# A two-layer convolution with a joint network on one core: first loads in a new order, tap 0 in two column parts, a leading tile of 456 columns, and a table of priority corrections

## The chip, the cores and the metric

The kernel runs on one core of one Trainium2 chip. The metric is device time of one execution in microseconds (us). Engines are named as in the profile: PE is TensorE (PEld its weight loads), DVE is VectorE, ACT is ScalarE, POOL is GpSimd, and SP is SyncE, whose queue issues every DMA of this kernel. The profiler was on for one execution; its span runs from the first instruction to the last.

## The reference

The input x has 2 sequences of 4000 samples with 512 channels. All tensors are bfloat16.

```python
B, T, D, K = 2, 4000, 512, 5;  U = 8
xp = jnp.pad(x, ((0,0),(pad,pad),(0,0)))                  # pad = 2
h = sum over i of einsum("btc,cd->btd", xp[:, i:i+T, :], w1[i])
h = gelu(h)[:, ::2, :]                                    # 2000 positions are kept
f = the same with hp = pad(h), w2
f = gelu(f)[:, ::2, :]                                    # 1000 positions are kept
fe = einsum("btd,de->bte", f, w_f);  ge = einsum("bud,de->bue", g, w_g)
j = tanh(fe[:, :, None, :] + ge[:, None, :, :])           # 2 x 1000 x 8 x 512
return einsum("btud,dv->btuv", j, w_o)
```

So there are two convolutions of five taps and stride 2, a small projection, a tanh over 16,000 rows of 512, and a 512 x 512 product on all of these rows.

## The kernel before

Everything is kept with channels on the 128 partitions (four groups of channels, index k) and positions along the row. The work runs in this order.

1. *The leading tile.* The first 2 x NA = 432 outputs of the first convolution in sequence 0 are made by plain products: for each tap (order 0, 4, 2, 1, 3) and each group m of 128 output channels, four products over k (`direct`, with the moving columns from `both`). All four banks of PSUM stay open over the five taps. The samples for it come as rows (`load_xr`, tiles `xr`, two blocks: 128 rows and the rest), are transposed by PE against `ident` (line 501 of the profile), and copied to `xs` by DVE (first block) or ACT (second block). A block holds samples in four phases (position modulo 4); the index pp says even or odd phases, and each block is transposed in two groups, pp = 0 and pp = 1. Taps 0, 4 and 2 read even phases only, taps 1 and 3 odd ones. Eight products on zeros (`warm_mm`, `NWARM`) go ahead of it on PE.
2. *The Triples.* The other outputs of the first convolution and the whole second one are made three output phases at a time by nine products in place of fifteen. Two Triples of N3 = 262 columns finish sequence 0 of the first convolution (inputs `xq`), two of 334 make sequence 1 (`xp`), and two make the second convolution (`hT`). They need sums of weights (`w1part`, `w2part`: tiles `ssum`, `w_x`, `w_t`) and sums of samples (`step`: tiles `row`, `xq`), made by DVE and ACT. Their samples come by transposing DMAs (`load_x6`, line 456 of the profile).
3. *The joint.* After the projection `fe` the tanh rows are made by ACT, and the last product is done in blocks of two by two with seven half-size products in place of eight (class `Seven`) and some plain tiles (`Plain`). The sums that a block of seven needs (line 912, tiles `ss`) run on DVE or POOL, whichever the planner picks; PSUM is emptied by DVE and ACT (`sn`, `og`, `ost`).

The order on each engine is not written by hand. Every step is an operation in a `Plan` with an engine (or a choice of two, `flex`), the tiles it reads and writes, and an assumed cost. `schedule` walks through the operations in assumed time: it takes the engine that is free first and, among operations that are ready, on PE, SP and POOL the one that comes first in the program, on DVE and ACT the one with the earliest due time `late`. Operations made while `pl.pin` is true (up to the end of the leading tile) keep the program's order on their engine. `emit` then writes each engine's fixed list with the semaphore waits that the order needs. Before the change the plan has 1631 operations.

DMAs of weights of the first convolution are held back so that few are under way: `load_w1` makes a load wait, on SP, for the landing of an earlier one (`came[-3]`). What stands behind it in SP's queue waits too, the transposed loads among them.

Of the kernel before, what the change touches and what calls it, by code (L numbers as in the profile page):

```python
# [50 lines left out]
class Psum:  # L51
# [4 lines left out]
        return View(self.h[:, lo:lo + n], np.unique(np.arange(lo, lo + n) // 512), True)  # L56

    def pair(self, lo, step, n):
        ap = self.h[:, lo:lo + 2 * step].rearrange("p (s c) -> p s c", s=2)[:, :, 0:n]
        cells = np.unique(np.concatenate([np.arange(lo, lo + n), np.arange(lo + step, lo + step + n)]) // 512)  # L60
        return View(ap, cells, True)


class Op:
    __slots__ = ("eng", "fn", "reads", "writes", "dma", "signal", "count", "sem", "val", "idx", "cost", "pin", "after", "wire", "alt", "port")


class Plan:
# [88 lines left out]
    def schedule(self, pred):  # L157
# [10 lines left out]
        for i in range(n - 1, -1, -1):  # L168
            t = min([late[s] - (HOP if pred[s][i] else ops[i].cost - span[i]) for s in succ[i]], default=0.0)
            if ops[i].eng == "pe":  # L170
                t = min(t, nextpe)
            late[i] = t - span[i]
            if ops[i].eng == "pe":
                nextpe = late[i]
        left = [len(p) for p in pred]
        ready = [0.0] * n
        free = {e: 0.75 for e in ("pe", "act", "dve", "pool", "sp")}
# [11 lines left out]
        for _ in range(n):  # L189
            best = None  # L190
            for e, c in cand.items():
                if c:
                    t = max(free[e], min(ready[i] for i in c))
                    if best is None or t < best[0]:
                        best = (t, e)
            t, e = best
            now = [i for i in cand[e] if ready[i] <= t + 0.02]
            i = min(now, key=(lambda i: i) if e in ("pe", "sp", "pool") else (lambda i: (late[i], i)))
            for f in engines(i):
                cand[f].remove(i)  # L200
            order[e].append(i)
            o = ops[i]
            if o.alt:
                o.eng, (o.fn, o.cost), o.alt = e, o.alt[e], None
            start[i] = t
            free[e] = t + o.cost
            if o.port:
                if lock > t - 0.2 and e == "dve":
                    free[e] = max(t, lock) + o.cost + 0.2
                elif lock > t:  # L210
                    free[e] = lock + o.cost
                lock = free[e]
            end = free[e]
            if o.dma:
                wire = max(wire, t + 1.8) + o.wire
                end = max(wire, t + 2.0)
            for s in succ[i]:
                ready[s] = max(ready[s], end + HOP if pred[s][i] else free[e])
                left[s] -= 1
                if not left[s]:  # L220
                    for f in engines(s):
                        cand[f].append(s)
# [79 lines left out]
def bass_standalone__seq2seq_rnn_t_joint__speech_kernel(  # L302
# [22 lines left out]
    NK = D // P  # L325
    assert (B, T, D, K, U) == (2, 4000, 512, 5, 8)
    T1, T2 = T // 2, T // 4
    NA, N3 = 216, 262
    NT3 = (T2 + 2) // 3
    XW = 528  # L330
    HOFF, HWID = 2, 338
# [1 line left out]
    RING, WIDE, XB = 12, 10, 24  # L333
    BU = B * U
    NT = 512
    NWARM = 8

    with ExitStack() as es:
        cur = [16512]
# [29 lines left out]
        assert cur[0] <= 229368, cur[0]  # L369
        xp = {i: Buf(nc, f"xp{i}", [6, NK, 352], BF16, xs[i].end - xs[i].bytes) for i in (0, 2)}  # L370
        assert all(xp[i].end <= xs[i].end for i in xp)
        xq = [Buf(nc, f"xq{i}", [6, NK, 288], BF16, v.end - v.bytes) for i, v in enumerate((xs[1], w2_sb))]
        assert xq[0].end <= xs[1].end and xq[1].end <= w2_sb.end
        w1_x = Buf(nc, "w1_x", [3, NK, D], BF16, wf_sb.end - wf_sb.bytes)
        assert w1_x.end <= wo_sb.end
# [30 lines left out]
        def memset(v):  # L406
            pl.op("pool", lambda e: e.memset(v.ap, 0.0), (), (v,))  # L407
# [11 lines left out]
        def mm(o, pairs, start, stop, check=True):  # L419

            def fn(e):
                for n, (l, r) in enumerate(pairs):
                    ins = e.matmul(o.ap, lhsT=l.ap, rhs=r.ap, start=start and n == 0,  # L423
                                   stop=stop and n == len(pairs) - 1, skip_group_check=not check)
                return ins
            pl.op("pe", fn, [v for pr in pairs for v in pr], (o,), len(pairs) * max(o.ap.free_size() / 2400 + 0.0025, 0.1))


        zv = zero[:]
# [12 lines left out]

        NR = (P, NA + 2 - P)

        def load_xr(rt):
            n = NR[rt]
            dst = xr[rt].rows(0, n).map(lambda a: a.rearrange("p r k c -> p (r k c)"))
            src = x[0, 4 * P * rt:4 * (P * rt + n), :].rearrange("(p r) c -> p (r c)", r=4)
            return pl.dma("sp", lambda e: e.dma_start(dst.ap, src), (), (dst,), nbytes=n * 4 * 2 * D)

        def load_x6(buf, b, ph, j0, col, n=336):

            r0 = b * T + 6 * j0 + ph
            dst = buf[ph, :, col:col + n]
            src = x.rearrange("b t d -> (b t) d")[r0:r0 + 6 * (n - 1) + 1:6, :]
            pl.dma("sp", lambda e: e.dma_start_transpose(out=dst.ap, in_=src), (), (dst,), nbytes=n * 2 * D, rate=170e3)  # L456

        came = [load_xr(rt) for rt in range(2)]
        act(warm[0:1], warm[1:2], ACT.Gelu_apprx_tanh)

        def load_w1(i):
            src = w1[i].rearrange("(k c) d -> c k d", c=P)
            if len(came) == 2:
                h = D // 2
                for sl in (slice(0, h), slice(h, D)):
                    o = pl.dma("sp", lambda e, sl=sl: e.dma_start(w1_sb[i, :, sl].ap, src[:, :, sl]), (), (w1_sb[i, :, sl],), nbytes=262144)
            else:
                o = load_w("sp", w1_sb[i], src)
                o.after.append(came[-3].idx)
            came.append(o)  # L470

        def load_xq(i, ph):
            load_x6(xq[i], 0, ph, 2 * NA // 3 + i * N3 - 2, 0, -(-(N3 + 3 - i) // 16) * 16)

        for kind, i in (('w', 0), ('w', 4), ('w', 2), ('w', 1), ('w', 3), ('x', 4), ('x', 0), ('x', 2), ('x', 1), ('x', 3), ('x', 5)):
            if kind == "w":
                load_w1(i)
            else:
                load_xq(0, i)
        for ph in (4, 0, 2, 1, 3, 5):  # L480
            load_xq(1, ph)
        for ph in (4, 0, 2, 1, 3, 5):
            load_x6(xp[2], 1, ph, 0, 16)

        def warm_mm(n):
            o, z, zz = ps.cols(3 * NT, NT), zero[0:P], zero[:]
            for _ in range(n):
                mm(o, [(z, zz)], True, True)
                pl.ops[-1].cost = 0.43

        warm_mm(NWARM)
        psb = ps.h[:, :].bitcast(BF16)
        for rt in range(2):
            for pp in range(2):
                bk, n = 4 + 2 * pp + rt, NR[rt]
                pv = View(psb[:, bk * 1024:(bk + 1) * 1024].rearrange("p (r k c) -> p r k c", r=2, k=NK)[:, :, :, 0:n], np.array([bk]), True)

                def fn(e, rt=rt, pp=pp, pv=pv, n=n):
                    for r in range(2):
                        for k in range(NK):  # L500
                            ins = e.transpose(pv.ap[:, r, k, :], xr[rt].h[0:n, 2 * r + pp, k, :], ident.h[0:n, 0:n])
                    return ins
                pl.op("pe", fn, (xr[rt].rows(0, n), ident[:]), (pv,), 0.55)
                o = xs[0][pp::2, :, 16 + rt * P:16 + rt * P + n]
                if rt:
                    act(o, pv, ACT.Copy)
                else:
                    pl.op("dve", lambda e, o=o, pv=pv: e.tensor_copy(out=o.ap, in_=pv.ap), (pv,), (o,), vec_cost(o, (pv,)))

        def stt(eng, o, a, f, b):  # L510
            pl.op(eng, lambda e: e.scalar_tensor_tensor(  # L511
# [139 lines left out]
        def to_f(b):  # L651
            def out(r, m, src):
# [5 lines left out]
        wb = {"t0": (w2_sb, 0), "s0": (w2_sb, 1), "t1": (w2_sb, 2), "s1": (w2_t, 2), "tm": (w2_t, 0), "t2": (w2_t, 1),  # L658
              "sm": (w2_t, 3), "si": (w2_sb, 3), "ti": (w2_sb, 4)}
        j3 = NA // 3  # L660
        trip = [Triple(xq[0], 2, row[0], wa, to_h(0, j3, N3), N3), Triple(xq[1], 2, row[1], wa, to_h(0, j3 + N3 // 2, N3), N3),
                Triple(xp[2], 16, row[0], wa, to_h(1, 0)), Triple(xp[0], 4, row[1], wa, to_h(1, NT3 // 2)),
                Triple(hT[0], HOFF, row[0], wb, to_f(0)), Triple(hT[1], HOFF, row[1], wb, to_f(1))]

        for b in range(B):
            memset(hT[b][4:6, :, HOFF - 1:HOFF])
            memset(hT[b][:, :, HOFF + NT3:HOFF + NT3 + 2])
        memset(xq[1][0:4, :, 1 + N3:4 + N3])  # L670
        memset(xq[1][4:6, :, N3:4 + N3])
        tap_at = {0: ((2, -1), (0, 0)), 1: ((3, -1), (1, 0)), 2: ((0, 0), (2, 0)),
                  3: ((1, 0), (3, 0)), 4: ((2, 0), (0, 1))}
        taps = (0, 4, 2, 1, 3)

        def both(i, k):

            a, b = (xs[0][r, k, 16 + d:16 + d + NA] for r, d in tap_at[i])
            lo, hi = a.ap, b.ap
            ap = bass.AP(tensor=lo.tensor, offset=lo.offset, ap=[list(lo.ap[0]), [hi.offset - lo.offset, 2], [1, NA]])  # L680
            return View(ap, np.union1d(a.cells, b.cells), False)

        def direct(i, m):
            mm(ps.cols(m * NT, 2 * NA), [(w1_sb[i, k, m * P:(m + 1) * P], both(i, k)) for k in range(NK)],
               i == taps[0], i == taps[-1])

        for i in taps:
            for m in range(NK):
                direct(i, m)
        for m in range(NK):  # L690
            src = ps.pair(m * NT, NA, NA).map(lambda a: a.rearrange("p s (q r) -> p s r q", r=3))
            o = hT[0][:, m, HOFF:HOFF + NA // 3].map(lambda a: a.rearrange("p (r s) q -> p s r q", s=2))
# [434 lines left out]
```

## Time and profile before

| what | value |
|---|---|
| time before, median of 3 runs | 253.12 us (252.08 to 253.51) |
| profiled execution: span | 251.3 us |
| profiled execution: PE busy | 245.7 us (98%) |
| DVE, ACT, POOL busy | 211.8, 210.5, 106.7 us |
| DMA, mean over the span | 127 GB/s |
| DMA from 6 to 12 us | 326 GB/s |
| granted TensorE clock, mean | 1.000 |

The page gives for the profiled execution its span alone, without a device time of its own; the three timed runs lie 0.8 to 2.2 us above that span. A busy share is a share of the span. Matmuls overlap one another in the records (their ends are modelled), so PE's busy time says where PE had work, and the spacing of matmul starts says how fast it went.

### The profile page before, as it was taken

Reading aid. Unit: us, or ns where it says so; the run is one execution under the profiler, and the core shown is the slowest. Engines: PE = TensorE matmul, PEld = TensorE weight load, DVE = VectorE, ACT = ScalarE, POOL = GpSimd, SP = SyncE. Lnnn points to the kernel's source line nnn. Section 1 sums busy time; section 2 is a strip of 40 time slices with the busy share of each in tenths; the row PEclk is TensorE's granted clock in tenths of the full one; section 3 lists DMA queues with packets and bytes.
Section 4 is the critical chain, followed back from the end, with each engine's and each line's share of the span. In section 5 each row is a group of like instructions: output and inputs, shape, how many; then the busy total and the mean of one; then the engine's idle time right before and its main releaser. Section 6 shows DMA issues by size and latency. Waiting matters only on the chain.

```text
span 251.3 us, 5205 instructions
## 1 busy us (share of the span) xinstructions
PE 245.7 (98%) x1920; PEld 184.6 (73%) x1920; DVE 211.8 (84%) x347; ACT 210.5 (84%) x353; POOL 106.7 (42%) x109
## 2 busy tenths in 40 slices
PE   8999999999999999999999999999999999999994
PEld 4556788877666666666467878777788888778873
DVE  1699999967999997971547798999999999999892
ACT  2388699878959869963799999999999999997763
POOL 1000000000000000003338899698998999699930
PEclk9999999999999999999999999999999999999999
DMA  7999999988400052000002223322344336534648
GB/s 212 326 174 176 186 156 208 176 144 274 148 0 3 0 182 71 1 1 3 0 1 85 83 86 127 127 86 83 127 132 164 128 120 219 187 123 148 207 137 266
DMA packets 57392, 31.92 MB, mean 127 GB/s; under 512 B 33837, under 2 KB 57149, under 8 KB 57367
## 3 DMA queue, kind: packets, MB, share of 16 engines
q1 hardware_dynamic: 57367, 31.59, 48.0%
q8 instruction: 15, 0.25, 0.4%
q14 instruction: 10, 0.08, 0.1%
HBM read 7.71 MB, written 16.38 MB: 96 GB/s over the span
## 4 chain that ended last, share of the span: by engine, by line
PE 85%; DMA 6%; DVE 5%; ACT 2%; SPq 1%; issue 1%; DVEq 0%
PE acc L423 85%; DMA xq<-in_x_dram 3%; DMA w_sb<-in_w_dram 2%; DVE row L410 2%; DMA xr<-in_x_dram 1%; DVE xq L410 1%; SPq L456 1%; ACT sn L843 1%; DVE og L410 0%; ACT jT L415 0%; DVE sn L844 0%; DVE ssum L511 0%; ACT ost L843 0%; DVE w_t L410 0%; DVE w_x L410 0%
## 5 line engine op out<-in xcount | busy, mean ns | idle before, releaser
L410 DVE TENSOR_TENSOR og<-acc,sn 128x512 bf16<-128x512 f32 x87 | 56.9, 681 | 3.9 <-PE acc L423 3.1
L415 ACT ACTIVATE jT<-feT,geT 128x1000 bf16<-128x1000 f32 (+6 forms) x56 | 51.7, 975 | 0.5 <-DVE feT L736 0.4
L423 PE MATMUL acc<-tw,ss 128*128 128x256 f16 x348 | 48.0, 273 | 0.0
L912 POOL TENSOR_TENSOR ss<-jT 128x512 f16<-128x512 bf16 x28 | 33.8, 1219 | 12.9 <-ACT jT L415 10.6
L423 PEld LDWEIGHTS acc<-tw,ss 128*128 128x128 f16 x348 | 33.5, 98 | 7.3 <-DVE sn L844 0.3
L843 ACT ACTIVATE sn<-acc 128x512 f32<-128x512 f32 x52 | 31.5, 620 | 3.5 <-PE acc L423 3.2
L423 PE MATMUL acc<-row,w_sb 128*128 128x334 bf16 (+1 forms) x192 | 33.1, 295 | 0.2 <-DVE row L410 0.2
L423 PE MATMUL acc<-wo_sb,jT 128*128 128x256 bf16 (+1 forms) x196 | 31.7, 288 | 0.0
L407 POOL MEMSET hT<- 128x8 bf16 (+2 forms) x6 | 0.7, 148 | 71.8 <-ACT hT L415 66.8
L423 PE MATMUL acc<-row,w_x 128*128 128x262 bf16 (+1 forms) x192 | 28.2, 290 | 0.0
L415 ACT ACTIVATE jX<-feT,geT 128x1000 bf16<-128x1000 f32 (+4 forms) x28 | 25.0, 932 | 0.0
L423 PEld LDWEIGHTS acc<-row,w_sb 128*128 128x128 bf16 x192 | 18.5, 98 | 6.8 <-DVE row L410 0.5
L423 PEld LDWEIGHTS acc<-wo_sb,jT 128*128 128x128 bf16 x196 | 19.2, 98 | 5.3
L423 PEld LDWEIGHTS acc<-row,w_x 128*128 128x128 bf16 x192 | 18.8, 98 | 5.4
L415 ACT ACTIVATE sd<-acc 128x334 f32<-128x334 f32 (+1 forms) x48 | 20.5, 431 | 1.9 <-PE acc L423 1.3
L912 POOL TENSOR_TENSOR ss<-jX 128x512 f16<-128x512 bf16 x18 | 20.9, 1176 | 1.2 <-ACT jX L415 0.7
L415 ACT ACTIVATE hT<-acc 128x262 bf16<-128x262 f32 (+2 forms) x36 | 15.1, 432 | 6.7 <-PE acc L423 6.6
L511 DVE SCALAR_TENSOR_TENSOR acc<-acc,sd 128x334 f32<-128x334 f32 (+1 forms) x24 | 11.6, 483 | 10.4 <-PE acc L423 10.3
L844 DVE COPY sn<-acc 128x512 f32<-128x512 f32 x25 | 16.9, 682 | 2.4 <-PE acc L423 2.2
L423 PE MATMUL acc<-wo_sb,ss 128*128 128x256 bf16 x116 | 17.9, 273 | 0.0
L423 PE MATMUL acc<-hT,w_sb 128*128 128x334 bf16 x96 | 17.4, 305 | 0.0
L912 POOL TENSOR_TENSOR ss<-ss,jT 128x512 f16<-128x512 f16 x14 | 16.4, 1181 | 0.7 <-PE acc L423 0.4
(105 smaller groups left out, 501.6 us busy)
## 6 DMA issues: line engine op xcount, KB each, us to landing
out_dram<-og SPq DMA_DIRECT2D x44, 256.0 KB, 2.3
w_sb<-in_w_dram SPq DMA_DIRECT2D x9, 512.0 KB, 5.0
out_dram<-og SPq DMA_DIRECT2D x14, 128.0 KB, 2.7
out_dram<-ost SPq DMA_DIRECT2D x7, 128.0 KB, 2.0
xr<-in_x_dram SPq DMA_DIRECT2D x1, 512.0 KB, 3.4
w_sb<-in_w_dram SPq DMA_DIRECT2D x2, 256.0 KB, 5.1
wf_sb<-in_w_f_dram SPq DMA_DIRECT2D x1, 512.0 KB, 3.6
wg_sb<-in_w_g_dram SPq DMA_DIRECT2D x1, 512.0 KB, 4.7
```

What stands on the lines that cost most here:

```text
L407: pl.op("pool", lambda e: e.memset(v.ap, 0.0), (), (v,))
L410: pl.op(eng, lambda e: e.tensor_tensor(out=o.ap, in0=a.ap, in1=b.ap, op=op), (a, b), (o,), 0.02 + 2.14e-3 * o.ap.free_size() if eng == "po ...
L415: pl.op("act", lambda e: e.activation(o.ap, i.ap, func, scale=scale, bias=0.0 if bias is None else bias.ap), rd, (o,), o.ap.free_size() * ...
L423: ins = e.matmul(o.ap, lhsT=l.ap, rhs=r.ap, start=start and n == 0, stop=stop and n == len(pairs) - 1, skip_group_check=not check)
L456: pl.dma("sp", lambda e: e.dma_start_transpose(out=dst.ap, in_=src), (), (dst,), nbytes=n * 2 * D, rate=170e3)
L511: pl.op(eng, lambda e: e.scalar_tensor_tensor(out=o.ap, in0=a.ap, scalar=f, in1=b.ap, op0=ALU.mult, op1=add), (a, b), (o,), vec_cost(o, (a ...
L843: pl.flex({"act": (lambda e: e.activation(o.ap, v.ap, ACT.Copy), 0.05 + n * 0.833e-3), "dve": (lambda e: e.tensor_copy(out=o.ap, in_=v.ap) ...
L844: "dve": (lambda e: e.tensor_copy(out=o.ap, in_=v.ap), 0.065 + n * 1.04e-3)}, (v,), (o,))
L912: fn = lambda e, o=S[i], x=x, y=y, op=op: e.tensor_tensor(out=o.ap, in0=x.ap, in1=y.ap, op=op)
```

## The change

Four things change together.

*First loads.* Each `xr` block is loaded in two transfers, even and odd phases. The order on SP becomes: block 0 even, tap 0's weights in two halves of channels (before: two halves of output columns), block 1 even, tap 4, block 0 odd, block 1 odd, taps 2, 1, 3. Tap 2 waits on SP for the landing of tap 4, tap 1 for block 0 odd, tap 3 for block 1 odd.

*Tap 0 in column parts.* After five warm-up products the first group of eight transposes (block 0, even) goes to PE and one more warm-up product follows. Tap 0 is then done for the 128 columns that this block gives (per output half), first for two groups of channels; then come the transposes of block 1 even, the other two groups of channels, and the same for the remaining columns. The transposes of the odd phases move ahead of tap 2. DVE copies both even groups, ACT both odd ones.

*Leading tile of 456 columns.* NA grows from 216 to 228, and the first two Triples have 258 columns for 262.

*A table.* `NUDGES` has one character for each of 1643 operations, from -3.2 to +3.1 in steps of 0.1 us. It is added to the priority by which `schedule` picks among ready operations: to the due time on DVE and ACT, and on SP and POOL to 0.15 times the place in the program. PE keeps the program's order. If the length of the table isn't the number of operations, zeros are used. Some assumed costs are altered as well, and the border memsets of `hT` and `xq` change places in the program.

```diff
+ALPHABET = "0123456789ABCDEFGHIJKLMNOPQRSTUVWXYZabcdefghijklmnopqrstuvwxyz_-"
+NUDGES = (
+    "WWWW ... WWWRP-PwH5QRK_xNvM0mR0_rMrCpnYWK"
...
+        nudge = [0.1 * (ALPHABET.index(c) - 32) for c in NUDGES] if len(NUDGES) == n else [0.0] * n
...
-            i = min(now, key=(lambda i: i) if e in ("pe", "sp", "pool") else (lambda i: (late[i], i)))
+            i = min(now, key=(lambda i: i) if e == "pe" else (lambda i: (0.15 * i + nudge[i], i)) if e in ("sp", "pool") else (lambda i: (late[i] + nudge[i], i)))
...
-    NA, N3 = 216, 262
+    NA, N3 = 228, (258, 258)
...
-    NWARM = 8
+    NWARM = 5
...
-        def load_xr(rt):
+        def load_xr(rt, pp):
             n = NR[rt]
-            dst = xr[rt].rows(0, n).map(lambda a: a.rearrange("p r k c -> p (r k c)"))
-            src = x[0, 4 * P * rt:4 * (P * rt + n), :].rearrange("(p r) c -> p (r c)", r=4)
+            dst = xr[rt].rows(0, n, slice(pp, 4, 2)).map(lambda a: a.rearrange("p r k c -> p r (k c)"))
+            src = x[0, 4 * P * rt:4 * (P * rt + n), :].rearrange("(p r) c -> p r c", r=4)[:, pp::2, :]
...
+        def load_w1(i, parts=1):
+            n = NK // parts
+            for k in range(0, NK, n):
+                src = w1[i, k * P:(k + n) * P].rearrange("(k c) d -> c k d", c=P)
+                dst = w1_sb[i, k:k + n]
+                o = pl.dma("sp", lambda e, dst=dst, src=src: e.dma_start(dst.ap, src), (), (dst,), nbytes=n * 131072)
+                if len(came) > 4:
+                    o.after.append(came[-3].idx)
+                came.append(o)
+
+        came = [load_xr(0, 0)]
+        load_w1(0, 2)
+        came.insert(2, load_xr(1, 0))
         act(warm[0:1], warm[1:2], ACT.Gelu_apprx_tanh)
+        load_w1(4)
+        for rt in range(2):
+            came.append(load_xr(rt, 1))
+        for i in (2, 1, 3):
+            load_w1(i)
...
         warm_mm(NWARM)
+        turn(0, 0, "dve")
+        warm_mm(1)
...
+        for q0, n in ((0, P), (P, NA - P)):
+            for ks in ((0, 1), (2, 3)):
+                for m in range(NK):
+                    mm(ps.pair(m * NT + q0, NA, n), [(w1_sb[0, k, m * P:(m + 1) * P], both(0, k, q0, n)) for k in ks],
+                       q0 == 0 and ks[0] == 0, False, False)
+                if q0 == 0 and ks[0] == 0:
+                    turn(1, 0, "dve")
+        for i in taps[1:]:
+            if i == 2:
+                turn(0, 1, "act")
+                turn(1, 1, "act")
+            for m in range(NK):
+                direct(i, m)
```

`turn(rt, pp, eng)` is the body of the loop over transposes of before as a function: eight transposes of block rt, group pp, on PE, and the copy to `xs` on the engine named.

## The prediction

> **What bounds the kernel now.** I read the page first, then TensorE's timeline of the first 32 us, the chain of waits, and then the waits and the timeline late in the span.
>
> From the page, the span and the busy times:
>
> ```profile
> span 251.3 us, 5205 instructions
> PE 245.7 (98%) x1920; PEld 184.6 (73%) x1920; DVE 211.8 (84%) x347; ACT 210.5 (84%) x353; POOL 106.7 (42%) x109
> ```
>
> PE is the bound. So the question is when its useful work begins, how many columns it streams, and where it stops in between. The timeline of PE alone (start, length, what, in brackets the idle time before it):
>
> ```profile
> 1.19 3.60 PE L423 MATMUL acc<-zero 128*128 128x512 bf16 x8 [1.19 <-DVE zero L430]
> 4.58 2.35 PE L501 MATMUL acc<-ident,xr 128*128 128x128 bf16 x32
> 7.47 14.81 PE L423 MATMUL acc<-xs,w_sb 128*128 128x432 bf16 x80 [0.54 <-ACT xs L415]
> 22.12 3.74 PE L423 MATMUL acc<-row,w_x 128*128 128x262 bf16 x32
> 25.77 1.96 PE L423 MATMUL acc<-xq,w_t 128*128 128x262 bf16 x16
> 27.57 1.06 PE L423 MATMUL acc<-row,w_x 128*128 128x262 bf16 x8
> 28.83 0.62 PE L423 MATMUL acc<-row,w_sb 128*128 128x262 bf16 x4 [0.20 <-DVE row L410]
> ```
>
> Useful products begin at 7.47. The 80 of the leading tile start every (22.12 - 7.47)/80 = 183 ns: 432 columns at 2.4 a nanosecond are 180, and 3 ns on top. I use columns/2.4 + 3 ns below. Between 22 and 29 us 56 products of 262 columns (112 ns, 6.3 us) take 6.7: about 0.45 is lost, most of it before 28.83, where PE waits for DVE.
>
> The same engine's transposes alone, in stretches of 0.6 us (in brackets how many):
>
> ```profile
> 4.60:5.20 0.60, 0.60 (x6) 0.60 (x6) 1.00 1.05 218
> 5.80:6.40 0.60, 0.60 (x14) 0.60 (x12) 1.00 1.19 296
> ```
>
> 128-column transposes come at 107 ns at first and at 56 ns later: PE runs at half rate until about 5.9 us, 4.7 us after its first matmul (the warm-up matmuls too: 3.4 us for eight of 512 columns, 427 ns each), whatever the clock column says.
>
> The chain of waits, in order of time:
>
> ```profile
> 0.74 3.43 DMA xr<-in_x_dram
> 4.19 4.75 DMA w_sb<-in_w_dram
> ...
> 9.37 2.09 SPq L456
> 11.46 0.05 issue
> 11.51 6.42 DMA xq<-in_x_dram
> ...
> 28.83 185.64 PE acc L423 x1464
> ```
>
> Samples, weights and the transposed samples come through one queue; DVE then prepares the first Triple until 28.8, and from there PE sets the end. The last loss is late: the waits between 195 and 235 us, and one DVE instruction beside a POOL instruction there (timeline).
>
> ```profile
> PEld acc L423 <- DVE og L410: 0.7, 1, 0.7
> PEld acc L423 <- DVE sn L844: 0.5, 2, 0.3
> ```
>
> ```profile
> 214.75 2.58 DVE L912 TENSOR_TENSOR ss<-jT,ss 128x512 f16<-128x512 bf16 x1
> 215.90 1.14 POOL L912 TENSOR_TENSOR ss<-jX 128x512 f16<-128x512 bf16 x1
> ```
>
> A sum that takes DVE 0.41 to 0.9 us elsewhere took 2.58 while POOL did sums too. PE's starts then stand 0.54, 0.21 and 0.11 us further apart than their columns need (218.5, 220.4, 226.7); with three small ones late stalls are 0.95 us. Early and late, 1.4 us of stall can be won, no more.
>
> **Part by part.**
>
> *First loads.* Now xr0 (512 KB) lands at 4.17, 3.43 after its issue. Afterwards the first transfer is half of it (256 KB, even phases). Its landing isn't in the trace; the nearest rows are 3.43 us for 512 KB above and 2.0 for a 128 KB store. I take 2.75, so it lands at 3.5 (bounds 2.75 to 4.2). Eight transposes at half rate (107 ns, 0.86 us, the first 0.17 after the landing) end at 4.5; DVE starts 0.24 later, as it does now (5.43 to 5.67), copies for 0.67 (1.33 for two), and 0.06 later PE can go: tap 0 starts at 5.5 (4.75 to 6.2), 2 us earlier. Its weights are the second and third transfer, 768 KB in all by 5.0 at the 350 GB/s at which 512 KB loads now follow each other (1.50 us apart), in time. Tap 4's weights have 0.42 MB less ahead of them: about 1.2 us earlier, 7.7, and PE wants them at 9.3. Taps 2, 1, 3 move behind the odd phases and wait on SP for tap 4 and for these; bytes in all grow by 49 KB (+0.15 us), while rows of 512 bytes disappear (tap 0's halves). So SP comes to the transposed loads at about 9 us, as now (9.37), and I let them land where they do, 17.94 for the second, within 0.6.
>
> *Tap 0 in parts.* 16 products become 32: 16 of 256 columns (110 ns) and 16 of 200 (86 ns), 3.14 us. The right part waits for the second transpose group and its DVE copy: eight transposes after the first eight products, at about 6.6 to 7.0, copy done at 7.8; eight left-part products (0.88) fill that time, so nothing waits. If the copy were 0.5 late, that much would show.
>
> *Transposes inside the stream.* 24 of 32 no longer lie ahead of the products: 8 of 102 columns, 8 of 128, 8 of 102 at 45, 56 and 45 ns, 1.17 us on PE's path. ACT's copies of the odd phases lie beside tap 2, which reads even phases only.
>
> *456 columns.* The other four taps: 64 x 193 ns = 12.35 us. The leading tile costs 3.14 + 12.35 = 15.49 against 14.65: +0.84. The first two Triples have 258 columns for 262: 288 products x 4 columns = -0.48. Their DVE and ACT rows get 1.5% shorter, beside other work.
>
> *Half rate.* 5.5 to 5.9 at half rate costs 0.2. Six warm-up matmuls for eight cost nothing by themselves; they keep the clock busy.
>
> Sum of the front: start -1.97, transposes +1.17, leading tile +0.84, half rate +0.2, Triples -0.48: **-0.25 us**. An early start is nearly all spent on work that used to lie before 7.47. Bounds of the landing make it -1.0 to +0.45.
>
> *DVE's lead.* DVE waits for tap 4's weights until 8.97 and is then without a pause but one of 0.43. After the change it can begin at about 8 (the copy ends at 7.8). The same rows then end up to 1 us earlier, and PE comes to the Triples at 22.4 instead of 22.1: the **0.45** early stall should go. It stays if the transposed loads are late by more than that.
>
> *Moved memsets.* The xq memsets wait for transposed loads until 31.5 on POOL; the hT memsets are now queued behind them. Nobody reads these borders before the second convolution, tens of us later: nothing.
>
> *The table.* It reorders DVE, ACT, POOL and SP after the pinned part. PE's order is fixed, so it can win only the 0.95 us of late stalls, and can lose without bound. DVE and POOL share the 116 sums of L912 (30 and 86); which fall together changes. I take two thirds won, **-0.65**, as nothing but the one long sum made most of it; bounds -0.95 to +3.
>
> Total -0.25 - 0.45 - 0.65 = -1.35: a span of 249.95. The profile gives the span alone; the runs (252.08 to 253.51) lie 0.8 to 2.2 above it, so I carry the difference to the median: 253.12 - 1.35 = **251.8**.
>
> **A rule weighed.** TensorE now reaches full rate at 5.9 although transposes fill the last 1.3 us before. The Trainium skill, TensorE: Matmul & The Clock Gate (Part 1 and Part 4), says that the clock rises only after a busy window of about 3.4 us, and that transposes don't count as busy. By that rule the pauses of the new start would keep the rate half to about 9.3, an estimate from the page's window, 1.7 us lost, and the total would be +0.35. The trace speaks half against it: the clock rose through those transposes.
>
> **The rivals.**
> - *The late stalls stay.* Front and early stall are won or only partly (-0.25 to -0.7), and new meetings of DVE and POOL replace the old. For: the runs of before spread by 1.4 us, as chance stalls would. Time 252.6.
> - *Half rate lasts longer (slower).* After the change PE pauses before the first transposes and about 0.55 us before tap 0. If that starts the 4.7 us again from 5.5, full rate comes at 10.2, and (10.2 - 5.9)/2 = 2.15 is lost: 253.9. It decides once more than 1.35, that is half rate beyond 8.6. Against: the pause of 0.74 between transposes and products at 6.7 doesn't drop the rate now. The page's rule weighed above is of this kind, and this is its chance.
> - *The new order jams the sums (slower).* One blocked sum cost PE 0.75 us (0.54 + 0.21). Against a gain of 0.7 in front, a second extra one makes the change lose; three make it slower by over 0.5%. Three to four: 255.0. For: ACT is busy without a pause from 160 to 220 and DVE nearly so, so lost time isn't made up. Against: the 30 sums on DVE met only one such block.
> - *The table does nothing.* It is used only if its length equals the number of operations. Before has 1631; two more sample loads, two fewer warm-ups and twelve more parts of tap 0 make 1643, which is its length, and every unpinned PE operation falls on a neutral W. Nearly excluded; 252.4.
>
> **How the numbers follow.** A measurement tells 0.5%, 1.27 us, from no change. Forecast 0.50, late stalls stay 0.22, half rate 0.10, jam 0.15, idle table 0.03. The forecast's own range is 250.6 to 252.7; 0.38 of its 0.50 lies below 251.85. Faster: 0.38 + 0.02 of the first rival = 0.40. Same: 0.12 + 0.20 + 0.07 of half rate + 0.03 = 0.42. Slower: 0.15 + 0.03 = 0.18. The range 250.5 to 254.6 leaves out most of the jam (0.12), the tail of half rate (0.03) and 0.05 below.
>
> **What would show it.** Right: first product of the leading tile at 5.5, the first Triple product at 22.4, no wait for DVE near 28, last matmul about 1.3 us before 248. Wrong: transposes or 256-column products at twice their length beyond 6 us; a gap before the 200-column part; DVE sums of over 2 us with PE waits behind them; or a landing of the first samples near 4.2, which would eat the front.

## The result, and the profile after

The changed kernel is slower: 255.41 us (median of 20 runs) against 253.0 for before in the same measurement (20 runs). The ratio is 1.0091, 95% interval 1.0072 to 1.0110, about 2.3 us; it leaves out one of the 20 runs, of 257.65 us at a granted clock of 0.987, which counts as slow. The forecast was 251.8, in a range of 250.5 to 254.6. In the runs of this study the device time lies 1.8 us above the span of the same execution, so spans can be compared directly: 254.3 after, 251.3 before. The profiled execution of after took 256.07, 0.7 above the median.

From the page of after:

```profile
span 254.3 us, 5220 instructions
PE 247.6 (97%) x1934; PEld 186.4 (73%) x1934; DVE 207.8 (82%) x346; ACT 209.3 (82%) x354; POOL 106.0 (42%) x109
```

PE still sets the time. Its timeline in the first 32 us (start, length, what, idle time before it and what ended it):

```profile
1.19 2.32 PE L444 MATMUL acc<-zero 128*128 128x512 bf16 x5 [1.19 <-DVE zero L451]
4.24 1.03 PE L523 MATMUL acc<-ident,xr 128*128 128x128 bf16 x8 [0.73 <-DMA xr<-in_x_dram]
5.06 0.63 PE L444 MATMUL acc<-zero 128*128 128x512 bf16 x1
6.06 1.89 PE L444 MATMUL acc<-xs,w_sb 128*128 128x256 bf16 x8 [0.36 <-DVE xs L530]
9.46 0.86 PE L523 MATMUL acc<-ident,xr 102*128 102x102 bf16 x8 [1.52 <-DMA xr<-in_x_dram]
10.12 6.86 PE L444 MATMUL acc<-xs,w_sb 128*128 128x256 bf16 x40
...
26.90 4.12 PE L444 MATMUL acc<-row,w_x 128*128 128x258 bf16 x36
```

Tap 0 does start earlier than the leading tile did before (6.06 against 7.47). But then PE waits for block 1 even until 9.46, and it works at half rate: the 40 products from 10.12 to the next transposes at 16.82 need 5.34 us at full rate (8 x 110 + 16 x 86 + 16 x 193 ns) and took 6.70, so full rate came about 2 x 1.36 = 2.7 us after 10.12, at 12.9. The first Triple product runs at 26.90 instead of 22.12, 4.8 us late.

The chain of waits names what PE waited for, and SP's queue what became late behind it:

```profile
2.62 6.79 DMA xr<-in_x_dram
```

```profile
...
4.12 1.43 SPq L470 DMA_DIRECT2D xr<-in_x_dram  x2
10.59 2.64 SPq L484 DMA_DIRECT2D w_sb<-in_w_dram  x3
13.27 8.30 SPq L477 DMA_TRANSPOSE xq<-in_x_dram  x4
```

A transfer of 204 KB took 6.79 us from its issue. After the two odd transfers SP stands still until 10.59, when tap 4's weights have landed (8.94 in before), and the transposed loads begin at 13.27 instead of 9.37. Meanwhile the DMA engines are partly idle (share of the 16 engines and GB/s in the last two columns):

```profile
10.00:10.50 0.50, 1.00 0.41 139
```

Behind the first Triple product the time fell by about as much as was hoped. From there to the start of the last matmul after takes 251.11 - 26.90 = 224.2 us, before 247.77 - 22.12 = 225.65 (whether the table did it, experiment 7 asks). Late waits of PE between 195 and 240 us are smaller than the 0.7 and 0.5 shown of before:

```profile
PEld acc L444 <- DVE og L431: 0.4, 2, 0.3
PEld acc L444 <- DVE sn L880: 0.2, 1, 0.2
```

### The profile page after: what moved, and what is told of

It is laid out like the page before. It is cut to its first block, busy times and chain, and to the rows that moved or that the text cites. A ratio compares the mean times of both kernels' runs of the same rounds, so it can differ in the third digit from the quotient of the medians.

```text
span 254.3 us, 5220 instructions
## 1 busy us (share of the span) xinstructions
PE 247.6 (97%) x1934; PEld 186.4 (73%) x1934; DVE 207.8 (82%) x346; ACT 209.3 (82%) x354; POOL 106.0 (42%) x109
## 4 chain that ended last, share of the span: by engine, by line
PE 95%; DMA 3%; SPq 1%; ACT 0%; issue 0%
PE acc L444 94%; DMA xr<-in_x_dram 3%; PE acc L523 1%; SPq L484 0%; SPq L470 0%; ACT ost L436 0%
## 5 line engine op out<-in xcount | busy, mean ns | idle before, releaser
L431 DVE TENSOR_TENSOR og<-acc,sn 128x512 bf16<-128x512 f32 x87 | 56.3, 680 | 5.4 <-PE acc L444 3.6
L444 PE MATMUL acc<-tw,ss 128*128 128x256 f16 x348 | 48.8, 273 | 0.0
L948 POOL TENSOR_TENSOR ss<-jT 128x512 f16<-128x512 bf16 x29 | 34.6, 1206 | 12.9 <-ACT jT L436 11.2
L879 ACT ACTIVATE sn<-acc 128x512 f32<-128x512 f32 x49 | 28.9, 615 | 1.6 <-PE acc L444 1.5
L444 PE MATMUL acc<-row,w_x 128*128 128x258 bf16 (+1 forms) x192 | 28.1, 289 | 0.0
L880 DVE COPY sn<-acc 128x512 f32<-128x512 f32 x28 | 19.1, 685 | 4.3 <-PE acc L444 4.1
L436 ACT ACTIVATE hT<-acc 128x258 bf16<-128x258 f32 (+2 forms) x36 | 15.2, 439 | 7.2 <-PE acc L444 7.2
L444 PE MATMUL acc<-xs,w_sb 128*128 128x456 bf16 (+2 forms) x96 | 18.2, 356 | 0.4 <-DVE xs L530 0.4
L444 PE MATMUL acc<-wo_sb,ss 128*128 128x256 bf16 x116 | 17.9, 273 | 0.0
```

Of the source, the lines that this page charges most:

```text
L431: pl.op(eng, lambda e: e.tensor_tensor(out=o.ap, in0=a.ap, in1=b.ap, op=op), (a, b), (o,), 0.02 + 2.14e-3 * o.ap.free_size() if eng == "po ...
L436: pl.op("act", lambda e: e.activation(o.ap, i.ap, func, scale=scale, bias=0.0 if bias is None else bias.ap), rd, (o,), o.ap.free_size() * ...
L879: pl.flex({"act": (lambda e: e.activation(o.ap, v.ap, ACT.Copy), 0.05 + n * 0.833e-3), "dve": (lambda e: e.tensor_copy(out=o.ap, in_=v.ap) ...
L880: "dve": (lambda e: e.tensor_copy(out=o.ap, in_=v.ap), 0.065 + n * 1.04e-3)}, (v,), (o,))
L948: fn = lambda e, o=S[i], x=x, y=y, op=op: e.tensor_tensor(out=o.ap, in0=x.ap, in1=y.ap, op=op)
```

## The experiments

Ratios are to the kernel before, with their 95% intervals; its median was 252.9 to 253.2 in these measurements.

**1. 102 rows in the changed kernel.** The transfers of block 1 become 112 rows.

```diff
-            n = NR[rt]          # 128, 102
+            n = (P, 112)[rt]
```

> The changed kernel, with the two transfers of block 1 made 112 rows long instead of 102 (ten rows more than are used). Theory (few DMA engines): 102 = 6 x 17 rows are spread over 6 of 16 engines, so a transfer of 209 KB lands 6.8 us after its issue and everything behind it waits; 112 = 16 x 7 rows use all. Then block 1 even lands before 6.5 us, tap 4's weights near 8, the gap of 1.5 us ahead of the second transposes goes, and the first Triple product starts at about 24.4 in place of 26.9; time 2 to 2.5 us below the changed kernel (255.4), about 253. Rival (pieces of 1 KB are slow whatever the rows): landing stays near 9.4 and the time within 0.5 us of 255.4. Second rival (only the half clock matters): gap gone, but the time falls by less than 1 us.

Measured 254.56 us, 1.0063 (1.0043 to 1.0082): 0.85 below the changed kernel. The first Triple product starts at 25.37. Block 1 even lands at 7.87 instead of 9.41, far from the 6.5 expected, and PE still waits 1.22 us for it (1.52). So the number of rows is a part of the loss, and not all of the late landing.

The rate went another way than in after. The first eight products of tap 0, from 5.65, took 1.05 us, which is full rate, and then the granted clock fell to half for 3.41 us (two stretches with PE's busy time; the granted clock is third from the end):

```profile
4.61:8.02 3.41, 1.62 (x15) 1.00 0.91 265
8.02:11.43 3.41, 3.41 (x24) 0.50 0.51 139
```

The 40 products that took 6.70 us in after took 6.77 here, so the 1.5 us that the first Triple product gained came from the earlier landing and not from the rate. The front itself doesn't fix the rate: in the profile of the same kernel with an empty table (experiment 7) the first eight products took 1.89 us, and full rate came at 9.3.

**2. The same row count on the kernel before.** Leading tile of 456 columns alone, with 102 and with 112 rows for block 1.

```diff
-    NA, N3 = 216, 262
+    NA, N3 = 228, 258
...
-            n = NR[rt]          # the second kernel alone
+            n = (P, 112)[rt]
```

> The kernel before with the leading tile of 456 columns alone (Triples of 258), all else as before; block 1 is then one transfer of 102 rows of 4 KB instead of 90. Theory (few DMA engines): 6 engines in place of 15 (90 = 6 x 15) carry 418 KB, 70 KB each, so it lands at about 8 to 9 us in place of 5.9, the leading tile starts at about 9.5 to 10.5 in place of 7.5, and the time is 2 to 3.5 us above before, 255.5 to 256.5. Rival (only rows cut into 1 KB pieces are slow): landing near 6.2, leading tile at 7.7, time within 0.7 us of before.

> The kernel before with the leading tile of 456 columns, and block 1 loaded with 112 rows instead of 102. Theory (few DMA engines): the whole 3.7 us that 102 rows cost goes; block 1 lands at about 6.0, the leading tile starts at 7.6; 252.9 to 253.6. Rival (the larger tile itself costs): above 254.5.

Measured 256.56, 1.0142 (1.0110 to 1.0174), with 102 rows, and 253.80, 1.0016 (0.9989 to 1.0043), with 112. PE's timelines, first of the one with 102 rows, then of the one with 112:

```profile
8.23 1.03 PE L501 MATMUL acc<-ident,xr 102*128 102x102 bf16 x16 [2.19 <-DMA xr<-in_x_dram]
9.71 16.86 PE L423 MATMUL acc<-xs,w_sb 128*128 128x456 bf16 x80 [0.44 <-ACT xs L415]
```

```profile
7.59 15.63 PE L423 MATMUL acc<-xs,w_sb 128*128 128x456 bf16 x80 [0.58 <-ACT xs L415]
```

Ten more rows of data make the kernel 2.8 us faster. Nothing else differs, so the row count is shown as a cause. With 102 rows the leading tile starts 2.1 us later, and its 80 products take 1.2 us more, as the granted clock was 0.50 from 8.9 to 12.3. 102 is 6 x 17, 112 is 7 x 16, and the 90 rows of before are 15 x 6. The Trainium skill, DMA: Bandwidth & Descriptors (the section on why a DMA increments its semaphore by 16 and not by 1), says that a transfer runs on the largest number of engines up to 16 that divides its outer dimension; that gives 6, 16 and 15. The traces agree. While block 1 was the transfer under way, from 3.6 to 4.2 us, the share of the 16 DMA engines (before the GB/s) was close to 6/16 = 0.375 with 102 rows, and full with 112:

```profile
3.60:4.20 0.60, 1.00 0.36 143
```

```profile
3.60:4.20 0.60, 1.00 1.04 410
```

The larger tile alone, with good rows, is not measurably slower than before, as its terms in the sum (+0.84 - 0.48) said.

**3. Pauses and half rate.** To the kernel with 112 rows: seven warm-up products ahead of the first transposes and two behind them.

```diff
-    NWARM = 5
+    NWARM = 7
...
-        warm_mm(1)
+        warm_mm(2)
```

> The kernel with 112 rows, and with two more warm-up products ahead of the first transposes and one more behind them, so that PE has no pause from 1.2 us to tap 0; the table is moved by three neutral places to stay on its operations. Theory (pauses kept TensorE at half rate until 12.9 us): full rate from about 6, tap 0's 256-column products at 110 ns from there, first Triple product at 22.7, a time of about 251.5 to 252, that is 1.2 to 1.7 us below the kernel with 112 rows and no extra warm-ups. Rival (the clock rises at the same time whatever fills the pauses): same as the kernel with 112 rows within 0.4 us.

Measured 255.76, 1.0124 (1.0078 to 1.0170), not faster than with 112 rows alone; its time was missed by 4 us. The rate did what was expected, but less of it was new than the theory says: eight 256-column products took 1.05 us (1.89 in after), as they did in experiment 1 without the extra products. New is that the rate stayed full behind PE's wait of 1.58 us for block 1, and the first Triple product came at 24.15 (25.37). But then PE ran into DVE, in an execution that took 257.78, 2 us more than the median of its four (timeline):

```profile
24.15 1.48 PE L445 MATMUL acc<-row,w_x 128*128 128x258 bf16 x12
27.76 3.31 PE L445 MATMUL acc<-row,w_x 128*128 128x258 bf16 x16 [2.12 <-DVE row L432]
```

The 16 products after that wait took 3.1 us, 0.19 each in place of 0.11: half rate again. The chain that ends this wait starts at the first transposed load, which landed at 20.06 (15.49 in before), and runs over ACT and DVE. In experiment 1 PE came 1.2 us later and didn't wait here, so what half rate had hidden came out. How much of the wait the other three executions had is not shown.

**4. The waits on SP.** The same kernel, holding taps 2, 1 and 3 back by earlier landings.

```diff
-                if len(came) > 4:
-                    o.after.append(came[-3].idx)
+                if i in (2, 1, 3):
+                    o.after.append(came[{2: 1, 1: 3, 3: 2}[i]].idx)
```

> The kernel with 112 rows and filled pauses, with the waits on SP loosened: tap 2 waits for the first half of tap 0's weights, tap 1 for the second half, tap 3 for block 1 even, instead of for tap 4 and the two odd blocks. Theory (the waits on SP let the DMA engines run dry from about 9.2 to 11.6 us and hold the transposed loads back to 12): the dry stretch goes, the first transposed load is issued at 8.3 to 9 in place of 12.1, DVE has its samples in time and the 2.1 us PE wait for DVE at 27.8 goes; time 253.5 to 254, some 2 us below the kernel with 112 rows and filled pauses (255.8). Rival (that wait comes from DVE's own work): the wait stays above 1.5 us and the time within 0.5 us of 255.8.

Measured 254.38, 1.0060 (1.0039 to 1.0081), 1.4 below the kernel of experiment 3 and a little above the 253.5 to 254 expected. The dry stretch of the DMA engines is gone, as the same stretch of experiment 3 and then of this one shows (share and GB/s last):

```profile
10.00:11.00 1.00, 1.00 0.12 34
```

```profile
10.00:11.00 1.00, 1.00 1.13 256
```

The transposed loads are issued from 8.71, and the wait of 2.1 us for DVE has shrunk to one of 0.7 for ACT. Part of the gain is still missing: the second transposed load lands at 19.6 (before: 17.9), and PE waits 0.74 us inside the leading tile for copies of odd phases.

**5. Loads in two pieces a row, on the kernel before.**

```diff
...
-        came = [load_xr(rt) for rt in range(2)]
+        came = [load_xr(rt, pp) for rt in range(2) for pp in range(2)][1::2]
```

> The kernel before with each block loaded in two transfers, even and odd phases, one after the other; everything else as before (block 1 keeps 90 rows). Theory (a transfer in two 1 KB pieces a row takes 0.6 to 0.7 us of SP instead of 0.39, and its first data come at 2.4 us in place of 1.6): block 0 complete at 4.7 to 5, leading tile starts at 7.9 to 8.3 in place of 7.5, weights 0.6 later; 0.4 to 0.9 us slower than before. Rival (the split costs nothing): within 0.3 us of before, first data at 1.6.

Measured 254.87, 1.0078 (1.0050 to 1.0107): 1.7 to 2 us, more than expected. SP's queue and PE:

```profile
0.73 3.36 SPq L449 DMA_DIRECT2D xr<-in_x_dram  x4
```

```profile
7.63 1.10 PE L501 MATMUL acc<-ident,xr 90*128 90x90 bf16 x16 [1.47 <-DMA xr<-in_x_dram]
8.99 15.98 PE L423 MATMUL acc<-xs,w_sb 128*128 128x432 bf16 x80 [0.26 <-ACT xs L415]
```

Four issues take SP 3.36 us where two took 0.91, everything behind them is later (the transposed loads start at 11.00, before at 9.37), and after the pause of 1.5 us on PE the granted clock was 0.50 from 8.0 to 11.4 (the 80 products take 15.8 us, before 14.65).

**6. Fewer warm-up products, on the kernel before.** `NWARM = 5` in place of 8, nothing else.

> The kernel before with five warm-up products in place of eight, nothing else, so that PE pauses from 3.3 us to the first transposes at about 4.2. Theory (a pause in the first microseconds puts off full rate by one more stretch of about 3.4 us in some or all runs): full rate at 8 to 12 us in place of 5.9, leading tile begins at 7.5 to 8.2 and ends 0.5 to 2 us later; 0.4 to 1.5 us slower than before. Rival (the clock counts only from the first product and pauses are harmless): within 0.3 us of before.

Measured 254.10, 1.0036 (1.0003 to 1.0069), in the middle of what was expected, with runs from 251.18 to 254.78. PE's timeline in an execution of 252.97:

```profile
4.16 3.09 PE L501 MATMUL acc<-ident,xr 128*128 128x128 bf16 x32 [0.65 <-DMA xr<-in_x_dram]
7.51 16.21 PE L423 MATMUL acc<-xs,w_sb 128*128 128x432 bf16 x80 [0.26 <-ACT xs L415]
23.55 3.74 PE L423 MATMUL acc<-row,w_x 128*128 128x262 bf16 x32
```

The 80 products take 16.04 us instead of 14.65, so half rate lasted until about 7.5 + 2 x 1.4 = 10.3. A pause of 0.65 us and earlier transposes, 2.8 us of them, are all that changed before that. So three missing warm-up products can be enough to put off full rate; they need not be, as in experiment 1 five products and a pause of 0.44 us left it full at 5.65. The Trainium skill, TensorE: Matmul & The Clock Gate (Part 4: PE-mode transpose), says that transposes don't count as busy for the clock in the way that products do; this run agrees, since 2.8 us of them didn't raise it, while in before 3.4 us of warm-up products ahead of them did. The pause of 0.65 us stands there too, and the run doesn't tell the two apart. The loss of 0.9 us is that of the medians. The execution shown reached the first Triple product 1.43 us later than before and made up 1.23 behind it (224.42 us to the last matmul, 225.65 before): PE no longer waits for DVE near 28, and DVE's long sum took 1.45 us here.

**7. The table.** Emptied in the changed kernel; emptied in the kernel with 112 rows; put, without its first twelve places, into the kernel before.

```diff
-NUDGES = ( ... )
+NUDGES = ""
```

> The changed kernel with an empty table, so that all corrections are zero. Theory (the front alone loses, the table is worth little): within 0.7 us of the changed kernel's 255.4, either side; first Triple product at 26.9 as with the table. Rival (the table's order jams the joint): 2 us or more faster than 255.4. Other rival (the table hides part of the loss): 1 us or more slower, with PE waits of over 1.5 us after 120 us.

> The changed kernel with block 1 in 112 rows and an empty table: the pair of the kernel with 112 rows (254.56). It settles what the table does in the changed kernel, where the run without it spread too far. Theory (the table wins 0.3 to 1 us of stalls behind the front): 254.9 to 255.6. Rival (nothing, as on the kernel before): 254.2 to 254.9.

> The kernel before with only the table (its first twelve neutral places dropped, since the plan has twelve operations fewer) and the altered assumed costs. Theory (the table is worth a part of the late stalls): 0 to 0.9 us below before, late PE stalls of about 0.5 us in place of 0.95. Rival (a table searched for another front jams): 1 us or more slower than before.

Measured 256.92, 1.0154 (1.0107 to 1.0201), beside 1.0091 with the table; 255.60, 1.0100 (1.0066 to 1.0134), beside 1.0063 with it; and 253.02, 1.0005 (0.9985 to 1.0026), on before. The time of the first would fit "the table hides part of the loss", but its trace, of the fastest of its four runs, has no waits of that size, and the four spread over 2 us; in both pairs the intervals touch or overlap, so by time alone the table's worth is 0 to 1.5 us. The traces say where it acts. Without the table (112 rows) the waits of PE late in the span are those of before again:

```profile
PEld acc L430 <- DVE og L417: 0.6, 1, 0.6
PEld acc L430 <- DVE sn L866: 0.5, 2, 0.3
```

DVE's long sum is there too (timeline):

```profile
216.57 2.56 DVE L934 TENSOR_TENSOR ss<-jT,ss 128x512 f16<-128x512 bf16 x1
```

Of the seven profiled kernels without the table five have a sum of 2.56 to 2.58 us at this place, and two one of 1.44 and 1.45 (the changed kernel with an empty table, without the waits, and the kernel of experiment 6); of the seven with the table none has a sum over 1.4. So the long sum goes with the missing table, though it doesn't come in every execution without it. What that is worth is not shown: from the first Triple product to the last matmul the changed kernel takes 224.2 us with the table and 223.95 with an empty one, the kernel with 112 rows 224.2 and 225.1. On the kernel before it brought no measured gain; in its trace the gap near 28 us had grown from 0.36 to 0.65.

**8. Whole rows, and a try to beat both.** First the changed kernel with whole-row loads, 112 rows, tap 0 still in parts; then the kernel before with the table, 96 rows, DVE copying both even groups, and two transposed loads ahead of tap 3.

```diff
...
-        came = [load_xr(0, 0)]
-        load_w1(0, 2)
-        came.insert(2, load_xr(1, 0))
+        x0 = load_xr(0)
+        load_w1(0, 0, 2)
+        x1 = load_xr(1)
+        w0 = load_w1(0, 2, 2)
...
```

> The changed kernel with the blocks loaded whole again (4 KB rows, block 1 with 112 rows), SP's order x block 0, first half of tap 0's weights, block 1, second half, then taps 4, 2, 1, 3 with the waits of before; the odd transposes follow the even ones of their block at once, eight warm-up products. Tap 0 stays in column parts, the tile at 456 columns, the table in place. Theory (the gain of the column parts was there, the loads ate it): first block lands at 4.2, tap 0 starts at about 6.1, block 1 lands by 7, first Triple product at 22.3 to 22.8, transposed loads issued from about 9.5; time 251.8 to 252.7, at or just below before. Rival (tap 0 in parts has no gain in it even with good loads): 253.5 or more.

```diff
...
-                if rt:
+                if pp:
                     act(o, pv, ACT.Copy)
...
-        ... ('w', 1), ('w', 3), ('x', 4), ('x', 0), ('x', 2) ...
+        ... ('w', 1), ('x', 4), ('x', 0), ('w', 3), ('x', 2) ...
```

> Meant to beat both: the kernel before with the table (twelve neutral places dropped), block 1 loaded with 96 rows (all 16 DMA engines, six rows unused), DVE copying both even groups and ACT both odd ones, and the first two transposed loads ahead of tap 3's weights on SP. Theory (front of before plus what the runs left over): leading tile starts at 7.2, second transposed load lands near 16.5 in place of 17.9, the early stall on DVE (0.45 us) and two thirds of the late stalls go; 252.0 to 252.5, 0.15 to 0.4% below before. Rival (DVE's own work bounds the first Triple, whatever lands earlier): within 0.3 us of before.

Measured 253.93, 1.0043 (1.0013 to 1.0072), and 253.51, 1.0020 (0.9996 to 1.0045). Neither beats before. With whole rows tap 0 starts at 6.42, but block 1, now behind half of tap 0's weights, lands at 7.8 (7 expected), the first Triple product runs at 23.23, and PE then waits 0.9 and 0.5 us for ACT. The time lies in the rival's range of 253.5 or more, but as block 1 was late again, the run doesn't settle whether tap 0 in parts has a gain in it. In the second kernel PE did start earlier, at 7.01, and reached the Triples at 21.66; its timeline then shows

```profile
29.44 0.62 PE L443 MATMUL acc<-row,w_sb 128*128 128x262 bf16 x4 [0.84 <-DVE row L430]
```

that is, the product that ran at 28.83 in before runs at 29.44. An earlier PE only waits longer: DVE's preparation of the first Triple sets that time. The samples were not what held it, since the second transposed load landed at 14.6 (17.9 in before). DVE's first weight sum began at 9.8 (8.97), when tap 4's weights landed.

## Why the prediction was wrong, point by point

The sum had three terms: front -0.25, early stall -0.45, late stalls -0.65. The front failed. The other two held in their sum, partly by luck.

- *First landing, 3.5 (bounds 2.75 to 4.2).* It was 4.19. Half the bytes in two pieces a row take as long as the whole (4.17); in the other kernels with such loads it was 3.86 to 4.25. Tap 0 started at 6.06 instead of 5.5: +0.56 us.
- *"So nothing waits" for the second block.* This is one of the two steps that failed most, and the half rate below is the other. The working gave the transfer of 102 rows no landing of its own. By its bytes, 204 KB behind the 768 KB that were to be there by 5.0, it would have been 5.6, and the transposes at 6.6 to 7.0 needed it by then. It ran on 6 engines, queued behind other transfers, and landed at 9.4. PE stood from 7.74 to 9.46: +1.72. With 112 rows it still landed at 7.87, so rows are not the whole cause; what the two pieces a row and the transfers ahead of it add is not told apart.
- *Half rate costs 0.2.* It cost about 2.5 us. The rival *half rate lasts longer* was the right mechanism, priced at 2.15 with full rate at 10.2 and given 0.10; full rate came at 12.9, behind the wait for block 1, a pause that the rival hadn't counted (with that wait at 0.22 us, in the kernel with 112 rows and an empty table, it came at 9.3). "Six warm-up matmuls for eight cost nothing" was wrong by itself: experiment 6 charges 0.9 us, with an interval of 0.1 to 1.7, for five instead of eight. The rule that was weighed pointed to a slower total; setting it at a chance of 0.10 because the clock had risen once during transposes was the misjudgement.
- *Start -1.97, transposes +1.17, leading tile +0.84.* The transposes and the tile were sized right per instruction; at half rate some took twice that. Together the front was +4.8 at the first Triple product, where 22.4 had been forecast: 0.56 + 1.72 + 2.3 make the difference of 4.5. Of the 4.8 us, 1.4 came back between there and the last matmul and 0.4 behind it, which leaves the 3.0 us by which the two spans differ.
- *SP comes to the transposed loads at about 9 us.* It came at 13.27. The waits for tap 4 and the odd blocks were named, but a stretch without any transfer was not priced; experiments 3 and 4 differ by 1.4 us in it, where PE isn't late anyway.
- *Tap 4's weights 1.2 us earlier, at 7.7.* They landed at 10.57, 1.6 later than before. The bytes ahead of them were fewer, as the working said, but the slow transfer of block 1 was among them; with 112 rows they landed at 9.65, still 0.7 later than before.
- *DVE's lead of 1 us.* It became a lag: DVE's first weight sum is at 10.87 in after (8.97 before), behind a copy that waited for block 1, and it couldn't have begun before tap 4's weights at 10.57. The early stall did go, but because PE came 4.8 us late.
- *Triples -0.48, early stall -0.45, late stalls -0.65.* Together -1.58 from the first Triple product on; measured 224.2 - 225.65 = -1.43. The early stall went for another reason than the one given, and the late share isn't shown to be the table's, since the same front with an empty table takes 223.95. The working also sized the long sum against 0.41 to 0.9 us elsewhere; five other sums of before took 1.19 to 1.42.
- *Rival of jammed sums, 0.15.* Nothing of it is in the trace of after, which has no sum over 1.4 us. An idle table is excluded by the order of the products: behind the 36 that start at 26.90, 24 with `w_t` follow in a row, and with an empty table 16.

What stays open is how the 2.3 us of time divide between row count, two-piece loads, SP's waits and pauses. They don't look additive: mending one (experiment 3) brought out the next. The version with three of them mended (experiment 4) is still at 1.006, and with whole rows at 1.0043.

## What to carry to other kernels

Size a transfer by how many DMA engines its row count lets it use as well as by its bytes; loading a few rows too many can be the faster choice (112 for 102: 2.8 us). Before moving the start of the bounding engine forward, ask what the engine behind it needs: here DVE's sums, the weights that they start from, and the transposed loads on the same queue set when the next stage can run, and a load moved ahead of them can move that stage back. Pauses in the first microseconds of PE can cost twice, once as waiting and again as half rate afterwards, so products on zeros that look idle may be paying for themselves.

## What the runs showed of the hardware

- Two 1 KB pieces a row instead of one of 4 KB: issue on SP 0.70 us instead of 0.39, and almost nothing moved in the first 2.5 us (2 GB/s after, 54 before):

```profile
0.00:2.50 2.50, 1.31 (x4) 1.00 0.01 2
```

- A transfer of 408 KB in 102 rows of 4 KB let PE's next transposes start at 8.23, where 448 KB in 112 rows had landed at 5.73.
- Half rate could return, and late: after the wait of 2.1 us at 25.6 in experiment 3 the granted clock was 0.51 from 28.0 to 31.5, and the products took twice their time. It also returned in experiment 1 (8.02 to 11.43), in experiment 2 with 102 rows (8.85 to 12.26) and in experiment 5 (7.99 to 11.40), each time for 3.41 us. In these three it fell 3.41 us after the rate had risen (4.61, 5.43, 4.57), in experiment 3 seven times 3.41 after (4.20; all by the record of the granted clock, which has no entry before the first rise, so that the column shows 1.00 there). In the 3.41 us ahead of each of the four falls PE was busy for 1.23 to 1.62 us.
- A pause as long can pass. In experiment 3 the wait of 1.58 us for block 1 lies across 7.61, which is 4.20 + 3.41; PE was busy for 2.21 us of the 3.41 before this mark and for 2.68 of the 3.41 after it, and the rate stayed. In after PE was busy for 1.89 us of the 3.41 before 9.47, and for all of the 3.41 from there to 12.88, where full rate came. So these traces fit a rate that is decided every 3.41 us by how busy PE was in that stretch. The limit for a fall must lie between 1.62 and 2.21 us of work; where is not shown.
